# Attention backward: 64-row tiles for scores and dP, a quarter of dS transposed on TensorE, casts on ScalarE

## The chip, the cores and the metric

The kernel runs on one core of a Trainium2 chip. The metric is the device time of one execution in microseconds (us). All times and profiles were taken on the chip. The kernel before took 3544.08 us (median of 2 runs, 3537.90 and 3550.26); its profiled run has a span of 3518.2 us.

In the profile PE is TensorE's matmuls, PEld its weight loads, DVE is VectorE, ACT ScalarE, POOL GpSimd, SP the queue that issues most DMAs. PEclk is the share of full speed that TensorE's clock was granted.

## The reference, cut to what matters

A transformer block (layer norm with modulation, attention with 32 heads of 16, squared-ReLU MLP), forward and backward, for 2048 tokens of width 512. Only the attention backward is changed. Per head, with P the unnormalised exponentials and dO, dP already scaled and shifted by row sums:

```python
S  = Q @ K.T                # scores, recomputed
P  = exp(S * scale)
dP = dO @ V.T               # a row-sum term is folded into two extra columns
dS = P * dP
dV += P.T @ dO;  dK += dS.T @ Q;  dQ += dS @ K
```

## The kernel before

A group g holds four heads, each in a strip of 32 partitions (16 real rows, two more for dP). A unit is two heads (a = 0, 1), 128 queries and 512 keys; there are 1024 units. The scores of one head are taken by a full 128-row matmul against a K tile in which only that head's strip is non-zero ("masked"). dQ needs dS transposed, which a DMA does for two units at a time (DMA_TRANSPOSE in the trace, median 2.60 us; called the crossbar here).

```python
for a in range(2):      # PE, 4 matmuls of 512 columns per unit
    nc.tensor.matmul(sts[a][:], lhsT=T["QT"][:, q], rhs=masked["KT"][2*jp+a][:, c0:c0+512], start=True, stop=True)
for a in range(2):
    nc.tensor.matmul(dp[:, a, :], lhsT=T["dOT"][:, q], rhs=masked["VT"][2*jp+a][:, c0:c0+512], start=True, stop=True)
for a in range(2):      # ACT
    nc.scalar.activation(pu[:, a, :], sts[a][:], ACT.Exp, scale=self.scale)
if len(pend) >= LAG:
    kv(pend.pop(0))     # PE, of two units earlier: 16 matmuls of 16 columns into acckv (dK, dV)
nc.vector.tensor_tensor(ds2[:, i], dp[:], pu[:], ALU.mult)      # DVE
# ... after two units (i = 0, 1):
nc.sync.dma_start_transpose(dsT[:], ds2[:].rearrange("p i a k -> p (i a k)"))   # crossbar
dq(pendq.pop(0))        # PE, of three pairs earlier: 16 matmuls of 16 columns into accq (dQ)
```

PSUM holds two score banks, two dP buffers of two banks, one bank for dK/dV, one for dQ. The order in which each engine issues its instructions is chosen by a scheduler at build time from what is written; it is fixed when the kernel runs.

The softmax here doesn't subtract the row's maximum and nothing guards it: scores larger than these inputs give would overflow.

## Time and profile before

From the page: first the busy tenths of TensorE and the granted clock in 40 slices of the span, then three groups (line, engine, operation, output<-input, shapes, count | busy us, mean ns | idle time before, and what ended it).

```profile
...
PE   5999998888876878487997979989799998999977
...
PEclk7999999999997989699998989999899999999998
...
L1172 ACT ACTIVATE pu<-st 128x512 bf16<-128x512 f32 x2048 | 1114.5, 594 | 573.7 <-PE st L1165 572.3
L1175 DVE TENSOR_TENSOR ds<-dp,pu 128x1024 bf16<-128x1024 f32 x1024 | 1245.8, 1222 | 391.1 <-ACT pu L1172 251.2
...
L1165 PE MATMUL st<-KTm,QTq 128*128 128x512 bf16 x2048 | 655.2, 384 | 8.0 <-issue 6.8
...
```

The backward attention is slices 19 to 38. The clock stands at 8 or above in all but three of the 40 slices. The next fence is the view by stretches for the whole stage (first to last exp) and for a regular part of it: microseconds, busy time and count of each engine, granted clock, DMA share, GB/s.

```profile
...
core 0: us, PE busy (x) PEld busy (x) DVE busy (x) ACT busy (x) POOL busy (x), PEclk, DMA share, GB/s
1648.00:3336.00 1688.00, 1536.60 (x28076) 1013.63 (x28584) 1295.67 (x1243) 1114.17 (x2048) 30.79 (x33) 0.97 1.08 173
2604.40:2619.40 15.00, 14.74 (x277) 9.89 (x280) 12.25 (x10) 10.85 (x21) 0.00 (x0) 1.00 1.20 188
...
```

The stage takes 1688 us, 1.65 us a unit, with TensorE busy 91% of it. In the regular stretch TensorE is busy 14.74 of 15.00 us. The view of waits shows what makes up the rest: waiting for the crossbar's dsT.

```profile
...
PEld L1139 <- DMA dsT<-ds: 162.4, 101, 9.0
PE accq L1139 <- DMA dsT<-ds: 122.4, 87, 8.1
...
```

The timeline of TensorE gives the cost of each piece from start to start:

```profile
...
2603.00 0.59 PE L1165 MATMUL st<-KTm,QTq 128*128 128x512 bf16 x2
2603.43 0.38 PE L1168 MATMUL dp<-VTm,dOTq 128*128 128x512 bf16 x1
2603.86 0.17 PE L1120 MATMUL acckv<-Qg,ds 128*128 128x16 bf16 x1
2603.88 0.17 PE L1122 MATMUL acckv<-dOg,pu 128*128 128x16 bf16 x1
...
```

Two scores start at 2603.00 and the first dP at 2603.43, so a 512-column matmul takes 0.215 us; the second dP of this unit has no record (the trace of before lacks 509 of its 2048 dP matmuls), which is why the next line stands 0.43 us on. The 16-column matmuls follow each other every 25 ns. Four of the first kind and 24 of the second (16 for dK/dV; 8 for dQ, counted at 27 ns) make 0.86 + 0.62 = 1.48 us a unit. The written duration (0.17 us) spans some seven such starts, so it is not what one costs.

| before | us a unit |
|---|---|
| stage / 1024 | 1.65 |
| TensorE, sum of start distances | 1.48 |
| crossbar, 2.9 us for two units | 1.45 |
| VectorE, one product | 1.22 |
| ScalarE, two exps | 1.09 |

### The profile page before, as it was taken

The page shows a single profiled execution, that of the slowest core. Times are in us where ns is not written, and L with a number is a line of the kernel's source. Part 1 is how long each engine was busy: PE and PEld are TensorE (multiplying, and loading weights), DVE is VectorE, ACT ScalarE, POOL GpSimd, SP SyncE. Part 2 cuts the span into 40 slices and gives each one's busy share as a digit, 9 for nine tenths or more (in the row PEclk, how much of TensorE's full clock was granted, in tenths as well). Part 3 has the DMA queues.
Part 4 walks back from the last instruction along what each step waited for, and adds up shares of the span by engine and source line. Part 5 has one row for each costly group of instructions (what it writes and reads, how often), then busy time and mean ns, then how long its engine had stood idle before and what let it go on. Part 6 is the DMA issues. An engine that isn't in the chain of part 4 may idle for free. (4 is left out here: it accounts for less than half of the span.)

```text
span 3518.2 us, 99351 instructions
## 1 busy us (share of the span) xinstructions
PE 3006.1 (85%) x42822; PEld 1747.5 (50%) x43588; DVE 1908.0 (54%) x2886; ACT 2347.3 (67%) x3545; POOL 251.4 (7%) x343
## 2 busy tenths in 40 slices
PE   5999998888876878487997979989799998999977
PEld 2455543333333333265664656656566665666633
DVE  6222220000004366355886868878687786888855
ACT  3999999999982334333765756756566675767633
POOL 3111110000001014311000000000000000000000
PEclk7999999999997989699998989999899999999998
DMA  3111110000013355655999999999999999999952
GB/s 119 63 50 50 45 38 12 12 6 12 5 49 139 113 196 192 189 154 131 174 179 155 178 162 172 176 174 175 161 175 183 176 178 159 180 178 173 176 185 65
DMA packets 1190469, 449.43 MB, mean 128 GB/s; under 512 B 1097354, under 2 KB 1161484, under 8 KB 1190028
## 3 DMA queue, kind: packets, MB, share of 16 engines
q1 hardware_dynamic: 1159900, 361.61, 57.5%
q0 software_dynamic: 21504, 71.71, 6.9%
q10 hardware_dynamic: 8624, 9.70, 0.8%
q8 instruction: 341, 5.59, 0.6%
q14 instruction: 100, 0.82, 0.1%
HBM read 106.83 MB, written 67.64 MB: 50 GB/s over the span
## 5 line engine op out<-in xcount | busy, mean ns | idle before, releaser
L1172 ACT ACTIVATE pu<-st 128x512 bf16<-128x512 f32 x2048 | 1114.5, 594 | 573.7 <-PE st L1165 572.3
L1175 DVE TENSOR_TENSOR ds<-dp,pu 128x1024 bf16<-128x1024 f32 x1024 | 1245.8, 1222 | 391.1 <-ACT pu L1172 251.2
L412 ACT ACTIVATE pu<-st 128x1024 bf16<-128x1024 f32 x1024 | 940.1, 1376 | 4.7 <-PE accbank L418 4.7
L1165 PE MATMUL st<-KTm,QTq 128*128 128x512 bf16 x2048 | 655.2, 384 | 8.0 <-issue 6.8
L409 PE MATMUL st<-QTm,KTq 128*128 128x512 bf16 x1864 | 566.7, 377 | 6.9 <-ACT pu L412 1.5
L1120 PEld LDWEIGHTS <-ds 128*128 128x128 bf16 x8192 | 502.4, 96 | 119.0 <-issue 8.3
L1120 PE MATMUL acckv<-Qg,ds 128*128 128x16 bf16 x8192 | 532.1, 170 | 25.8 <-issue 2.9
L1122 PE MATMUL acckv<-dOg,pu 128*128 128x16 bf16 x8192 | 528.0, 169 | 0.0
L1122 PEld LDWEIGHTS <-pu 128*128 128x128 bf16 x8192 | 460.4, 96 | 118.3 <-issue 8.4
L418 PEld LDWEIGHTS <-pu 128*128 128x128 bf16 x8192 | 291.2, 96 | 458.7 <-ACT pu L412 408.2
L1168 PE MATMUL dp<-VTm,dOTq 128*128 128x512 bf16 x1539 | 508.7, 385 | 0.5 <-DMA dOTq<-dOTq_d 0.5
L418 PE MATMUL accbank<-Vaug,pu 128*128 128x17 bf16 x8192 | 353.5, 172 | 93.4 <-ACT pu L412 38.1
L1139 PE MATMUL accq<-Kg,dsT 128*128 128x16 bf16 x8192 | 311.8, 170 | 125.2 <-DMA dsT<-ds 123.1
L1139 PEld LDWEIGHTS <-dsT 128*128 128x128 bf16 x8192 | 263.5, 96 | 192.4 <-DMA dsT<-ds 164.6
L1168 PEld LDWEIGHTS <-dOTq 128*128 128x128 bf16 x2048 | 188.4, 97 | 244.7 <-issue 81.3
L427 DVE RECIPROCAL rl<-accbank 128x4 f32<-128x4 f32 x128 | 23.0, 180 | 526.0 <-PE accbank L418 525.6
L288 DVE TENSOR_SCALAR ev_fm<-pps,bcol 128x512 bf16<-128x512 f32 x92 | 69.1, 751 | 195.4 <-PE pps L281 185.7
L409 PEld LDWEIGHTS <-KTq 128*128 128x128 bf16 x2048 | 129.7, 96 | 35.4 <-issue 20.5
L1165 PEld LDWEIGHTS <-QTq 128*128 128x128 bf16 x2048 | 128.9, 96 | 11.1 <-issue 8.1
L281 PE MATMUL pps<-xhat1T,wpad 128*128 128x512 bf16 x372 | 119.9, 378 | 7.8 <-DVE ev_fm L288 3.8
L1104 POOL DMA_DIRECT2D QTq<-QTq_d x8 | 4.5, 558 | 1184.0 <-PE dp L1168 1156.4
L544 ACT ACTIVATE rT<-ups,bias 128x512 bf16<-128x512 f32 x56 | 38.5, 687 | 52.1 <-PE ups L542 52.0
(298 smaller groups left out, 2260.2 us busy)
## 6 DMA issues: line engine op xcount, KB each, us to landing
dsT<-ds SPq DMA_TRANSPOSE x512
rT_d<-rT SPq DMA_DIRECT2D x4, 1792.0 KB
rT<-rT_d SPq DMA_DIRECT2D x4, 1792.0 KB
duT_d<-duT POOLq DMA_DIRECT2D x4, 1792.0 KB, 12.0
rT_f<-rT_d SPq DMA_DIRECT2D x14, 512.0 KB
duT_f<-duT_d POOLq DMA_DIRECT2D x14, 512.0 KB, 4.1
xhat_d<-xhat SPq DMA_DIRECT2D x2, 2048.0 KB
QTq_d<-ev_fm POOLq DMA_DIRECT2D x32, 128.0 KB, 2.1
```

The costliest lines, as they stand in the source:

```text
L281: nc.tensor.matmul(pt[:, :sw], lhsT=wpads[t][:, kt, g, :], rhs=xhat1T[:, kt, s0:s0 + sw], start=(kt == 0), stop=(kt == DT - 1))
L288: nc.vector.tensor_scalar(ev[:, :sw], pt[:, :sw], bc, None, ALU.add)
L409: nc.tensor.matmul(stt[:, a, :qw], lhsT=KT[:, kb * P:(kb + 1) * P], rhs=QTm[a][:, q0:q0 + qw], start=True, stop=True)
L412: nc.scalar.activation(pu[:, :, :qw], stt[:, :, :qw], ACT.Exp, scale=self.scale)
L418: nc.tensor.matmul(acc[:, a, sub, :], lhsT=pu[:, a, sub * P:(sub + 1) * P], rhs=Vaug[:, kb, heads[a], :], start=False, stop=False, skip_gr ...
L1120: nc.tensor.matmul(acc[:, 0, a, sub, :], lhsT=ds[:, a, sub * P:(sub + 1) * P], rhs=T["Q"][:, ib, col:col + DH], start=False, stop=False, s ...
L1122: nc.tensor.matmul(acc[:, 1, a, sub, :], lhsT=pu[:, a, sub * P:(sub + 1) * P], rhs=T["dO"][:, ib, col:col + DH], start=False, stop=False, ...
L1139: nc.tensor.matmul(accq[:, ib0 + i, a, :], lhsT=dsT[:, (i * 2 + a) * 4 + sub, :], rhs=T["K"][:, 4 * c + sub, col:col + DH], start=False, s ...
L1165: nc.tensor.matmul(sts[a][:], lhsT=T["QT"][:, q], rhs=masked["KT"][2 * jp + a][:, c0:c0 + 512], start=True, stop=True)
L1168: nc.tensor.matmul(dp[:, a, :], lhsT=T["dOT"][:, q], rhs=masked["VT"][2 * jp + a][:, c0:c0 + 512], start=True, stop=True)
L1172: nc.scalar.activation(pu[:, a, :], sts[a][:], ACT.Exp, scale=self.scale)
L1175: nc.vector.tensor_tensor(ds2[:, i], dp[:], pu[:], ALU.mult)
```

## The change

The intent: TensorE and the crossbar are both nearly full, so relieve both. Scores and dP of a unit use opposite halves of the rows (heads are stored shifted by two strips for dO and V), as two 64-row tiles meant to run side by side. A quarter of the transposes goes from the crossbar to TensorE and VectorE. One dP in five is cast to bf16 by ScalarE, which makes VectorE's product all-bf16. K and V loads leave the transposes' queue.

```diff
-        LAG, LAGQ = 2, 3
+        LAG, LAGQ = 2, 4
 # ... K and V: two zeroed tiles each, by parity of the head, double buffered by group, loaded on the GpSimd queue
+    def turn(u):
+        (ds2, dsT) = u
+        tp = dpp.tile([P, 16, P], BF16, name="dp")          # a dP buffer
+        src = ds2[:].rearrange("p i a (s k) -> p (i a s) k", k=P)
+        for k in range(16):
+            nc.tensor.transpose(tp[:, k, :], src[:, k, :], self.ident[:])
+        nc.vector.tensor_copy(dsT[:], tp[:])
 # ...
+    rs, rd = slice(64 * jp, 64 * jp + 64), slice(64 * (1 - jp), 64 * (1 - jp) + 64)
     for a in range(2):
-        nc.tensor.matmul(sts[a][:], lhsT=T["QT"][:, q], rhs=masked["KT"][2 * jp + a][:, c0:c0 + 512], ...)
-    for a in range(2):
-        nc.tensor.matmul(dp[:, a, :], lhsT=T["dOT"][:, q], rhs=masked["VT"][2 * jp + a][:, c0:c0 + 512], ...)
+        nc.tensor.matmul(sts[a][:], lhsT=T["QT"][rs, q], rhs=T["KT", a][rs, ck], start=True, stop=True)
+        nc.tensor.matmul(dp[:, a, :], lhsT=T["dOT"][rd, q], rhs=T["VT", a][rd, ck], start=True, stop=True)
 # ...
-    nc.vector.tensor_tensor(ds2[:, i], dp[:], pu[:], ALU.mult)
+    if nu % 5 == 2:
+        nc.scalar.copy(ca[:], dp[:])
+        nc.vector.tensor_tensor(ds2[:, i], ca[:], pu[:], ALU.mult)
+    else:
+        nc.vector.tensor_tensor(ds2[:, i], dp[:], pu[:], ALU.mult)
 # ...
-    nc.sync.dma_start_transpose(dsT[:], ...)
+    while pendt: turn(pendt.pop(0))
+    if nt % 4 == 3: pendt.append((ds2, dsT))
+    else: nc.sync.dma_start_transpose(dsT[:], ...)
 # ... in kv(): the matmul with pu now stands ahead of the one with ds
```

## The prediction

> **What bounds it now.** The first and last ScalarE exp of the backward attention start at 1648 and 3335 us, so this stage holds 1024 units (two heads x 128 queries x 512 keys) in 1688 us: 1.65 us each, 48% of the span. Everything else is unchanged by the diff. In that window (view by stretches) TensorE is busy 91%, VectorE 77%, ScalarE 66%, and the DMA engines are full (share 1.08).
> Two limits lie close together. In the regular stretch 2604 to 2619 us a pair of units takes 3.00 us and TensorE is busy 98%: from start distances in the timeline, four 512-column matmuls at 0.215 us, 16 dK/dV matmuls at 25 ns and 8 dQ matmuls at 27 ns give 1.48 us a unit. The other limit is the crossbar: one transpose of a pair's dS holds the queue 2.9 us of those 3.0 (2.60 median), and the masked K/V loads, 0.3 to 0.5 us each, share that queue. When it falls behind, TensorE waits: 123 us plus 165 us of weight loads wait for dsT (view of waits; they overlap), which makes 1.65 out of 1.48.

> **What the change does, per unit.**
> - DMA: a quarter of the transposes and all masked loads leave this queue: 2.9 x 0.75 / 2 = 1.1 us. No longer a limit; the waits for dsT should almost vanish.
> - TensorE: [...]Score and dP use opposite 64-row halves, but only neighbours in the issue order can overlap. In the order of the built kernel the 4096 such matmuls fall into 1444 runs: 344 alternate fully, some 250 are SS,DD (half the gain), over 700 hold only scores or only dP. In-order overlap saves 0.23 us of 0.86. Transposes add 16 x 56 ns (eight take 0.61 us in the feed-forward stage) per 8 units: +0.11.[...]
> - VectorE: 0.8 x 1.245, plus 0.2 x 0.7 for all-bf16 products (estimate from 0.43 us at 512 columns), plus about 1.2/8 to evacuate transposes (0.69 us at 1024 columns), plus 0.07 of small work: 1.36.
> - ScalarE: 1.09 + 0.2 x 1.0 = 1.3.

> So all three engines come to 1.3 to 1.5 us, and the order of two shallow PSUM rings, one of them also lent to the transposes, costs something: I expect 1.50 us a unit, about 150 us less in the stage, nearly all of it on the critical path.

> **Prediction:** 3390 us (range 3270 to 3530). Faster by over 2%: 0.72; within 2%: 0.16; slower: 0.12.

> **What the profile would show.** Waits of TensorE for dsT fall from 288 us to under 80; DMA share in the stage falls from 1.08 to about 0.85; in alternating runs S and D start within about 20 ns of each other, and other runs stay at 0.215 us per matmul;[...] VectorE is 85 to 92% busy, ScalarE 80 to 88%; the stage takes about 1535 us.

> **What would make it wrong.**[...] The transposes hold a dP buffer through matmuls and copy and can stall the dP ring once in eight units. The first group's loads move to the GpSimd queue and may delay the start by some us.

Cut from it are statements that no trace or run of this case had shown, and with them terms of the sum. TensorE's terms that are left come to 1.48 - 0.23 + 0.11 = 1.36 us a unit; the cut term is my guess at what changing between 64-row and 128-row matmuls costs, and with it the sum came to about the 1.50 us a unit of the forecast. That the two halves overlap, on which the 0.23 rests, was itself an assumption then; the trace after shows it (1069 of the 4096 matmuls start within 30 ns of the one before, near the 1093 that counting opposite neighbours in the issue order gives).

## The result, and the profile after

The changed kernel took 4169.24 us (median of 2 runs, 4168.29 and 4170.18): 17.6% slower, ratio 1.1764 (95% interval 1.1675 to 1.1853). Ratios here are the mean time of one kernel's fast runs over that of the other's of the same rounds, so not quite the ratio of the medians quoted.

The page's lines of the changed kernel that answer to those of before:

```profile
...
PE   5999988888578686999999999999999999999987
...
PEclk8999999999789898555555555555556555555578
...
L1189 ACT ACTIVATE pu<-st 128x512 bf16<-128x512 f32 x2048 | 1125.9, 597 | 998.2 <-PE st L1185 825.6
L1197 DVE TENSOR_TENSOR ds<-dp,pu 128x1024 bf16<-128x1024 f32 x819 | 999.9, 1223 | 497.6 <-ACT pu L1189 263.6
L1185 PE MATMUL st<-KT,QTq 64*128 64x512 bf16 x2048 | 1027.4, 584 | 29.7 <-issue 24.2
...
L1195 DVE TENSOR_TENSOR ds<-ca,pu 128x1024 bf16<-128x1024 bf16 x205 | 141.8, 692 | 324.0 <-ACT ca L1194 324.0
...
L1194 ACT CAST ca<-dp 128x1024 bf16<-128x1024 f32 x205 | 208.3, 1016 | 35.8 <-PE dp L1186 35.6
...
```

The second line is the finding: from slice 17 on the clock row reads 5. The score matmul's mean duration is 584 ns, against 384 before. The exps, products, casts and the all-bf16 product last what was expected of them (597, 1223, 1016 and 692 ns). The stage as a whole, in the same columns as before (busy time PE, PEld, DVE, ACT, POOL, then clock, DMA share, GB/s):

```profile
...
1665.00:3984.00 2319.00, 2304.93 (x30602) 1167.36 (x30602) 1348.74 (x1369) 1304.32 (x2253) 59.87 (x92) 0.55 0.55 97
...
```

2319 us, 2.26 us a unit, at a mean clock of 0.55. TensorE is busy 99% of it, DMA only 0.55. So the relief of the crossbar came as intended: TensorE's waits for dsT shrank from 285 to 18 us. The line below is from the view of what the dQ matmuls waited for: the wait's end, then its microseconds and how often.

```profile
...
  DMA dsT<-ds: 17.7, 6
...
```

And the tiles run side by side as intended. TensorE's timeline, in a stretch at the half clock:

```profile
...
2602.77 0.60 PE L1186 MATMUL dp<-VT,dOTq 64*128 64x512 bf16 x1
2602.78 0.61 PE L1185 MATMUL st<-KT,QTq 64*128 64x512 bf16 x1
2603.17 0.63 PE L1186 MATMUL dp<-VT,dOTq 64*128 64x512 bf16 x1
2603.18 0.63 PE L1185 MATMUL st<-KT,QTq 64*128 64x512 bf16 x1
2603.74 0.19 PE L1132 MATMUL acckv<-dOg,pu 128*128 128x16 bf16 x1
2603.79 0.17 PE L1134 MATMUL acckv<-Qg,ds 128*128 128x16 bf16 x1
...
2604.16 0.17 PE L1134 MATMUL acckv<-Qg,ds 128*128 128x16 bf16 x1
2604.27 0.60 PE L1185 MATMUL st<-KT,QTq 64*128 64x512 bf16 x1
```

Score and dP start 10 ns apart (5 ns is the median of such pairs in the trace), but the 512 columns take twice as long: two neighbouring pairs start 0.40 us apart where it was 0.215. The last pair starts at 2603.18 and the first dK/dV matmul only at 2603.74, and from the last dK/dV matmul (2604.16) to the next score is 0.11 us, where narrow matmuls follow each other every 27 ns: the change between 64-row and 128-row matmuls costs time in both directions (0.56 against 0.40 us, 0.11 against 0.03).

TensorE's work a unit, from start distances of this trace, adds up like this. Of 4096 score and dP matmuls, 1093 are hidden behind a partner, as I counted in the built order (in the trace 1069 start within 30 ns of the one before):

| us a unit | at the full clock | at the half clock |
|---|---|---|
| 3003 places of 512 columns | 0.63 (0.215 each) | 1.20 (0.41 each) |
| 24 narrow matmuls | 0.60 (25 ns) | 0.65 (27 ns) |
| transposes, 2 a unit | 0.11 (56 ns) | 0.21 (107 ns) |
| 1444 round trips between the modes | 0.24 (170 ns) | 0.30 (216 ns) |
| sum | 1.58 | 2.36 |

The measured 2.26 lies close to the right column; the trace's clock records say that 222 us of the stage, in 32 stretches of 3.4 to 17.1 us, ran at the full clock. Weighting the two columns with that share gives 2.25.

### The profile page after: what moved, and what is told of

It reads as the page before. It is cut to its first block, busy times and chain, and to the rows that moved or that the text cites. A ratio compares the mean times of both kernels' runs of the same rounds, so it can differ in the third digit from the quotient of the medians.

```text
span 4166.5 us, 103731 instructions
## 1 busy us (share of the span) xinstructions
PE 3811.6 (91%) x45636; PEld 1904.7 (46%) x45636; DVE 1961.0 (47%) x3014; ACT 2537.5 (61%) x3750; POOL 282.3 (7%) x407
## 5 line engine op out<-in xcount | busy, mean ns | idle before, releaser
L1197 DVE TENSOR_TENSOR ds<-dp,pu 128x1024 bf16<-128x1024 f32 x819 | 999.9, 1223 | 497.6 <-ACT pu L1189 263.6
L1185 PE MATMUL st<-KT,QTq 64*128 64x512 bf16 x2048 | 1027.4, 584 | 29.7 <-issue 24.2
L1186 PE MATMUL dp<-VT,dOTq 64*128 64x512 bf16 x2048 | 1002.9, 587 | 0.0
L1134 PEld LDWEIGHTS <-ds 128*128 128x128 bf16 x8192 | 494.6, 104 | 182.9 <-issue 182.9
L1195 DVE TENSOR_TENSOR ds<-ca,pu 128x1024 bf16<-128x1024 bf16 x205 | 141.8, 692 | 324.0 <-ACT ca L1194 324.0
L1148 PE MATMUL dp<-ident,ds 128*128 128x128 bf16 x2048 | 237.7, 310 | 0.1
L1194 ACT CAST ca<-dp 128x1024 bf16<-128x1024 f32 x205 | 208.3, 1016 | 35.8 <-PE dp L1186 35.6
L1148 PEld LDWEIGHTS <-ds 128*128 128x128 bf16 x2048 | 205.8, 145 | 46.8 <-issue 46.5
L1149 DVE COPY dsT<-dp 128x2048 bf16<-128x2048 bf16 x128 | 156.7, 1224 | 140.1 <-PE dp L1148 131.5
L1185 PEld LDWEIGHTS <-QTq 64*128 64x128 bf16 x2048 | 141.0, 104 | 59.7 <-issue 35.3
L1186 PEld LDWEIGHTS <-dOTq 64*128 64x128 bf16 x2048 | 137.6, 105 | 54.3 <-issue 39.7
```

The lines of the kernel that those rows point to most:

```text
L1134: nc.tensor.matmul(acc[:, 0, a, sub, :], lhsT=ds[:, a, sub * P:(sub + 1) * P], rhs=T["Q"][:, ib, col:col + DH], start=False, stop=False, s ...
L1148: nc.tensor.transpose(tp[:, k, :], src[:, k, :], self.ident[:])
L1185: nc.tensor.matmul(sts[a][:], lhsT=T["QT"][rs, q], rhs=T["KT", a][rs, ck], start=True, stop=True)
L1186: nc.tensor.matmul(dp[:, a, :], lhsT=T["dOT"][rd, q], rhs=T["VT", a][rd, ck], start=True, stop=True)
L1194: nc.scalar.copy(ca[:], dp[:])
```

## The experiments

What lowered the clock? Theory 1: the clock follows how much the array is used, and the overlapped half-height matmuls use it too little. Rival 2: the transposes on TensorE lower it. Rival 3: the mode changes cost the time, and the clock is secondary. Kernels marked "single run" were run once, profiled, beside a run of before on the same chip; effects of 3% and more are read from them; a smaller one is a hint only. e4 and e12 to e15 gave wrong values.

### e1: the tiles alone

The kernel before with the 64-row matmuls and their loads, without transposes on TensorE, without casts, lags as before. Issue order as in before, only score and dP alternate.

```diff
-  if nu % 5 == 2:        # casts
+  if False:
-  if nt % 4 == 3:        # TensorE transposes
+  if False:
```

> The kernel before with only the 64-row score and dP matmuls (and the K/V loads that go with them): no TensorE transposes, no ScalarE casts, the lags and dK/dV order of before. Theory 1 (clock: overlapped 64-row matmuls leave the array too little active, and the granted clock falls to one half): mean clock in the backward attention 0.5 to 0.65, a unit 1.8 to 1.95 us, in all about 3700 to 3850 us. Rival 2 (the PE transposes lower the clock): clock above 0.9, 3300 to 3400 us. Rival 3 (the mode changes alone cost the time, the clock is secondary): clock above 0.9 and about 3500 to 3700 us.

3829.43 us against 3518.04 (single run). The stage:

```profile
...
1663.00:3647.00 1984.00, 1920.16 (x28593) 941.73 (x28592) 1308.89 (x1243) 1119.20 (x2048) 59.22 (x91) 0.50 0.86 147
...
```

Clock 0.50 throughout, 1.94 us a unit. No transpose runs on TensorE in it, so rival 2 falls.

### e2: the same tiles, nothing overlaps

e1 with dO and V loaded into the same half as Q and K.

```diff
-  rd = slice(64 * (1 - jp), 64 * (1 - jp) + 64)
+  rd = slice(64 * jp, 64 * jp + 64)        # dOT and VT loaded with their halves exchanged
```

> As e1, same issue order, same 64-row mode and mode changes, but score and dP of a unit use the same half of the rows, so nothing overlaps. Theory 1a (activity is the time in which anything streams): clock above 0.9 again, matmuls 0.215 us apart, about 3500 to 3650 us, faster than e1 though nothing overlaps. Theory 1b (activity is weighted by rows in use): clock 0.5, a unit near 2.5 us, about 4400 us. Rival 2: clock above 0.9. Rival 3: slower than e1 by the lost overlap at full clock, 0.3 us a unit.

4547.52 us (single run).

```profile
...
1662.00:4362.00 2700.00, 2661.47 (x28559) 1164.02 (x28558) 1310.75 (x1242) 1201.61 (x2048) 63.19 (x98) 0.50 0.60 108
...
```

The matmuls now follow one another 0.40 to 0.43 us apart; TensorE streams 4 x 0.41 of 2.64 us, a larger share than the 0.86 of 1.65 of before, and the clock stays at one half. So time in which something streams is not what counts (theory 1a falls); a matmul over 64 rows counts less than one over 128 (1b). Counted in columns rather than time the case is closer; the windows below settle it.

### e3: every pair twice

e1 with each score and dP matmul issued twice, the second overwriting the first.

```diff
   for a in range(2):
+      for _ in range(2):
           nc.tensor.matmul(sts[a][:], ...); nc.tensor.matmul(dp[:, a, :], ...)
```

> As e1, but every overlapped score/dP pair is issued twice (the second run of each overwrites the first, the result stays right): twice the matmul work. Theory 1: the activity is that of before again, clock above 0.9, a unit about 1.6 us, 3450 to 3650 us: more work, less time than e1. Rivals 2 and 3: slower than e1 by 0.4 us a unit, about 4200 us or more if the clock stays at one half.

3667.18 us (single run): twice the score and dP matmuls, 162 us less than e1, though 17 us above the range expected.

```profile
...
1664.00:3483.00 1819.00, 1749.20 (x32680) 1049.15 (x32680) 1309.72 (x1242) 1113.59 (x2048) 58.47 (x90) 0.98 0.94 161
...
```

The clock is 0.98. This refutes rival 3: the mode changes are nearly the same (the trace of e3 has 1022 runs of 64-row matmuls, that of e1 1226), and the 204 fewer, at 0.2 us each, are some 40 of the 162 us. TensorE's timeline of e3 shows the tiles at the full clock:

```profile
...
2602.17 0.38 PE L1186 MATMUL st<-KT,QTq 64*128 64x512 bf16 x1
2602.17 0.38 PE L1187 MATMUL dp<-VT,dOTq 64*128 64x512 bf16 x1
2602.38 0.38 PE L1186 MATMUL st<-KT,QTq 64*128 64x512 bf16 x1
2602.39 0.38 PE L1187 MATMUL dp<-VT,dOTq 64*128 64x512 bf16 x1
2602.70 0.18 PE L1132 MATMUL acckv<-Qg,ds 128*128 128x16 bf16 x1
2602.73 0.17 PE L1134 MATMUL acckv<-dOg,pu 128*128 128x16 bf16 x1
...
```

Pairs 0.21 us apart, and from the last pair (2602.38) to the first narrow matmul 0.31 us. The medians over the stage: 308 ns against 215 without a mode change, and 102 ns against 25 on the way back: 93 + 77 = 170 ns for the round trip. At the half clock (e1) the same steps take 563 and 107 ns, 136 + 80 = 216 ns beyond the 427 and 27 that before shows at its own half-clock moments.

### e4: less streaming without any tile

The kernel before, 128 rows everywhere, with score and dP matmuls of 256 columns that the consumers read twice.

```diff
-  nc.tensor.matmul(sts[a][:], ..., rhs=masked["KT"][2 * jp + a][:, c0:c0 + 512], ...)
+  nc.tensor.matmul(sts[a][:, :256], ..., rhs=masked["KT"][2 * jp + a][:, c0:c0 + 256], ...)   # dP alike
```

> The kernel before, full 128-row mode, no transposes on TensorE, but score and dP matmuls stream 256 columns instead of 512 and the consumers read those twice (wrong numbers on purpose). Theory 1: less streaming alone lowers the granted clock in the stage to 0.5 to 0.7, with no 64-row tile in it; the time stays about that of before, 3450 to 3600 us. Rivals 2 and 3 (the row tiles' mode changes or the transposes are needed): clock stays above 0.9, TensorE busy under 75% in the stage, and about 3350 to 3500 us.

3737.66 us (single run), later than expected; the product was also split in two here.

```profile
...
1642.00:3550.00 1908.00, 1628.37 (x28551) 1295.64 (x28550) 1360.21 (x2262) 1122.75 (x2048) 31.23 (x34) 0.50 0.90 153
...
```

Clock 0.50 without a 64-row matmul or a transpose in the stage. Half the columns do what half the rows did.

### e5: the loads on another queue

The kernel before, its masked loads issued from GpSimd.

```diff
-  nc.sync.dma_start(masked[n][j][r:r + 32, c0:c0 + cw], ...)
+  nc.gpsimd.dma_start(masked[n][j][r:r + 32, c0:c0 + cw], ...)      # backward only
```

> The kernel before, with its masked K and V loads of the backward attention issued from the GpSimd queue instead of the queue of the crossbar transposes. If the transposes fall behind because these loads and their waits block their queue, the waits of TensorE for dsT fall from 288 us to under 150 and the time falls by 50 to 130 us (3410 to 3490). If the crossbar itself is the limit, nothing changes (within 1%).

3528.38 us against 3549.11, ratio 0.9946 (0.9921 to 0.9971). The waits for dsT stayed (176 us of weight loads and 129 us of matmuls in the view of waits, against 165 and 123). The loads on the transposes' queue were not what held it up.

### e6: everything but the tiles

The changed kernel with 128-row masked matmuls.

```diff
-  nc.tensor.matmul(sts[a][:], lhsT=T["QT"][rs, q], rhs=T["KT", a][rs, ck], ...)
+  nc.tensor.matmul(sts[a][:], lhsT=T["QT"][:, q], rhs=masked["KT"][2 * jp + a][:, c0:c0 + 512], ...)   # dP alike
```

> The changed kernel with full 128-row score and dP matmuls (masked operands as before): a quarter of the transposes on TensorE, the casts, the lags and order of the change. Theory 1: clock above 0.9 in the stage; TensorE has 1.48 plus 0.11 us of work a unit, so about the time of before, 3450 to 3600 us. Rival 2: clock near 0.55, 4000 us or more.

3517.22 us against 3549.11, ratio 0.9913 (0.9892 to 0.9934).

```profile
...
1648.00:3330.00 1682.00, 1652.69 (x30622) 1133.68 (x30619) 1322.56 (x1372) 1283.30 (x2253) 31.31 (x35) 0.99 0.79 134
...
```

Clock 0.99. Transposes on TensorE, casts and the new lags are worth 0.9% together; the tiles, with the K and V loads that go with them, are the whole loss.

### e7: the change without TensorE transposes

```diff
-  if nt % 4 == 3:
+  if False:
```

> The changed kernel without the TensorE transposes (all on the crossbar). Theory 1: clock stays 0.5 to 0.65; saves the transposes' 0.2 us a unit at half clock: about 3900 to 4000 us. Rival 2: clock above 0.9, 3400 us or less.

3925.76 us (single run).

```profile
...
1660.00:3738.00 2078.00, 2035.58 (x28565) 961.68 (x28565) 1197.92 (x1242) 1310.73 (x2253) 59.48 (x92) 0.50 0.83 141
...
```

As expected: still the half clock (0.50), and cheaper by 243 us, near the transposes' time there (0.21 us a unit, 215 us).

### e8 and e9: a useless matmul more

The changed kernel with one full-height matmul more per unit, into the bank that the score overwrites; 256 and 512 columns.

```diff
+  nc.tensor.matmul(sts[0][:, :256], lhsT=self.ident[:], rhs=T["QT"][:, 0:256], start=True, stop=True)   # e9: 512
   for a in range(2):
```

> The changed kernel with one useless matmul more per unit: full 128 rows, 256 columns, into the score bank that the real score then overwrites (right result). Activity theory (the granted clock follows columns streamed times rows in use in each 3.4 us window): raised by 256 of about 1660 columns a unit, the stage leaves the half clock for most of the time, clock above 0.85, a unit about 1.5 to 1.6 us, in all 3400 to 3550 us: more work, over 600 us less. If the mode changes were the cost: slower than the changed kernel, 4200 us or more.

> As e8 with a useless matmul of 512 columns. Activity theory: clock above 0.95, a unit 1.6 to 1.7 us, 3480 to 3620 us; slower than e8 if e8 already holds the full clock, faster than e8 if it does not.

e8: 3717.75 us, e9: 3652.26 us (single runs), against 4169 for the change. The stage of e8, then of e9:

```profile
...
1663.00:3534.00 1871.00, 1840.02 (x31637) 1049.03 (x31635) 1338.54 (x1369) 1284.56 (x2253) 59.71 (x91) 0.88 0.70 121
...
```

```profile
...
1662.00:3469.00 1807.00, 1755.52 (x31633) 1009.62 (x31630) 1335.24 (x1369) 1280.90 (x2253) 59.40 (x91) 0.99 0.73 125
...
```

More work, 451 and 517 us less, with the clock at 0.88 and 0.99. Both came out above the expected time: the clock did what theory 1 said, but a unit took 1.83 and 1.76 us where 1.5 to 1.6 and 1.6 to 1.7 were expected. The scheduler also alternates more pairs in these (729 and 856 runs of two overlapped pairs in the traces, against 465 in the changed kernel), so part of the gain may be order; e1, with 862 such runs at the half clock, shows that order alone does not bring the clock back.

### e10: half of the transposes on TensorE

```diff
-  if nt % 4 == 3:
+  if nt % 2 == 1:
```

> The changed kernel with half of dS transposed on TensorE instead of a quarter. If TensorE transposes count as activity: the clock rises clearly over the 0.55 of the changed kernel (0.7 or more in the stage) and the time falls below 4000 us although TensorE has 0.1 to 0.2 us a unit more to do. If transposes do not count as activity: clock at 0.55 or below and 4300 us or more.

4441.99 us (single run).

```profile
...
1662.00:4260.00 2598.00, 2591.94 (x32680) 1371.74 (x32679) 1501.23 (x1497) 1308.43 (x2253) 60.84 (x93) 0.58 0.44 61
...
```

Between the two expectations (0.58 against 0.55), so inconclusive by itself. The windows below decide it.

### e11: e1 with the useless matmul

The line added in e8, put into e1.

> e1 (64-row tiles alone, no TensorE transposes, no casts; it never left the half clock) with the useless 256-column matmul of e8. Activity theory: about 1660 columns a unit, at the half clock some 2900 a window, close to where the clock recovers, so it may stay locked at 0.5 (then about 3950 us) or escape (clock above 0.9, about 3400 to 3500 us, the crossbar then the limit). Mode-change theory: clock 0.5 whatever is added.

3705.52 us (single run) against 3829 for e1.

```profile
...
1664.00:3521.00 1857.00, 1775.52 (x29588) 898.43 (x29588) 1300.61 (x1242) 1116.93 (x2048) 58.97 (x90) 0.71 0.95 158
...
```

The clock escapes, but only in part: 0.71.

### What the clock follows

```
columns x rows/128     window at full clock          window at half clock
in the window          next half   next full         next half   next full
under 2500             163         0                 2254        0
2500 to 3000           112         27                1786        38
3000 to 3500           42          267               259         173
3500 and more          0           4813              1           117
```

A window that holds under 2500 is never followed by the full clock, and one with 3500 or more is followed by it in all but one case of 4931, from either clock. The border lies near 3000 to 3300 columns, against some 8100 that fit (512 in 0.215 us). The best single limit mistakes 59 of the 5424 windows at full clock. If a 64-row matmul is counted at 0.4, 0.5 or 0.6 of a 128-row one, it mistakes 63, 59 and 82; counted in full, 196. If the transposes are left out it mistakes 228, and if the zero columns of e12 to e18 (below) are left out, 144. So rows count, at about one half for 64 of 128, and so do transposes on TensorE and columns of zeros. This also settles e2: without the rows, 155 of its windows hold 3500 columns or more, and none of them is followed by the full clock. Some records are missing (509 dP matmuls in before), which may explain part of the blurred border; what the hardware counts in detail is not shown.

With that, columns per unit explain the stages (sum per unit, over the measured time of a unit, times 3.413):

| kernel | columns a unit | us a unit | columns a window | clock |
|---|---|---|---|---|
| before | 2432 | 1.65 | 5036 | 0.97 |
| after | 1664 | 2.26 | 2508 | 0.55 |
| e1 | 1408 | 1.94 | 2480 | 0.50 |
| e2 | 1408 | 2.64 | 1822 | 0.50 |
| e4 | 1408 | 1.86 | 2579 | 0.50 |
| e11 | 1664 | 1.81 | 3132 | 0.71 |
| e8 | 1920 | 1.83 | 3587 | 0.88 |
| e9 | 2176 | 1.76 | 4209 | 0.99 |
| e3 | 2432 | 1.78 | 4673 | 0.98 |

For before that is 4 x 512 + 24 x 16; for after 4 x 512 / 2 + 24 x 16 + 256 for the transposes. The state feeds itself: at the half clock the changed kernel does not issue enough columns to leave it (2508 a window over the stage). A burst of 16 transposes can lift it: all 32 lifts of the changed kernel follow a window with eight or more transposes, though only one in four of its 128 such windows brings a lift. Then the stretch without transposes falls back.

### e12 to e15: columns at no cost

If columns count, they can be had nearly free: at the full clock a dK/dV matmul starts 25 ns after the last with 16 columns (before) and with 48 (e12). At the half clock it does not come free: 27 ns with 16, 40 ns with 48. Q and dO are kept in tiles with zero columns between the heads, and each matmul streams 48 columns, 32 of them zeros that add nothing to neighbouring accumulators.

```diff
-  nc.tensor.matmul(acc[:, 0, a, sub, :], lhsT=ds[...], rhs=T["Q"][:, ib, col:col + DH], ...)
+  nc.tensor.matmul(o[:, lo * DH:(lo + 3) * DH], lhsT=ds[...], rhs=wideQ[:, ib, r0 * DH:(r0 + 3) * DH], ...)   # dV alike
```

e12 is the change with this, e13 is e1 with this, e14 is e12 without casts, e15 is e12 without TensorE transposes.

> The changed kernel with its dK/dV matmuls made 48 columns wide (16 real ones, 32 zero columns that add nothing; right result). Such a matmul starts 25 to 27 ns after the one before[...]. If activity is columns streamed, zeros too, this raises it by 512 columns a unit at almost no time: clock above 0.9, a unit 1.4 to 1.55 us, 3300 to 3480 us, faster than before. If narrow or zero columns do not count: clock 0.55, about 4100 us.

> e1 (64-row tiles alone) with the 48-column dK/dV matmuls of e12. Activity theory: 1920 columns a unit, clock above 0.8 against 0.50 for e1, at or under 3500 us with the crossbar as the limit (1.45 us a unit). If narrow or zero columns do not count: 0.5 and 3830 us like e1.

> e12 without the ScalarE casts. Clock above 0.9 as e12; VectorE then has 1.245 + 0.15 + 0.07 = 1.47 us a unit, ScalarE 1.09: if the casts are worth what the prediction gave them, 0.03 to 0.1 us a unit slower than e12 (3380 to 3550 us).

> e12 without the TensorE transposes. Clock 0.8 to 1.0; crossbar at 1.45 us a unit is the limit, TensorE has 0.11 us less: 3380 to 3550 us. If transposes on TensorE are what lifts the clock out of its low state, it stays lower than e12's.

All four gave a relative error of 0.11 in the gradient of the QKV weights: I had placed the copy into a padded tile ahead of the last lagged dK/dV matmuls that still read it. Times (single runs; before took 3531.23): e12 3633.18, e13 3589.74, e14 3600.55, e15 3511.10 us. The stage of e12:

```profile
...
1679.00:3452.00 1773.00, 1647.11 (x30609) 1036.46 (x30607) 1316.86 (x1369) 1278.64 (x2253) 74.99 (x106) 0.96 0.74 127
...
```

From 0.55 to 0.96 with not one matmul more in the stage. The clock in the stages of e13, e14, e15 was 0.89, 0.96 and 0.94. e15 is faster than e12 by 122 us: once the clock is full, the transposes on TensorE cost about their 0.11 us a unit (113 us) and buy nothing. e14 is faster than e12 by 33 us, a hint that the casts cost too. The clock was as expected; the times of e12, e13 and e14 lie 153, 90 and 51 us above the ranges expected.

### e16, e17 and e18: right values, and what the other two parts are worth

e16 is e15 with the copy moved behind those matmuls and half of the clearing given to VectorE. e17 puts one transpose of eight on TensorE. e18 is e16 without casts.

```diff
+  if Tn is not None and jp == 0 and c == 1:
+      widen(Tn, g + 1)                # was in load_group
-  if False:                           # e17: if nt % 8 == 7:
-  if nu % 5 == 2:                     # e18: if False:
```

> e15 with its fault mended: the padded copies of Q and dO are now written after the last lagged dK/dV matmuls of the group that used them, so the result must be right; half of the clearing goes to VectorE, so the stage should start some 20 us earlier. Activity theory: clock above 0.9 in the stage as in e15, 3450 to 3520 us, 1 to 2.5% faster than before; the same kernel with 16-column dK/dV matmuls (e7) took 3926 us at the half clock. If the wrong values had anything to do with e15's clock: back to the half clock.

> e16 with one of eight transposes on TensorE. If the crossbar is what still limits e16, the waits of TensorE for dsT fall and it is 1% faster than e16; if the dP buffer lent to the transposes is what made e12 120 us slower than e15, half of that comes back: 50 to 60 us slower than e16.

> e16 without the ScalarE casts. VectorE then has 1.245 + 0.07 = 1.32 us a unit, ScalarE 1.09, the crossbar 1.45 as in e16. If the casts pay once the clock is full, as the prediction had it (0.1 us a unit less on VectorE): 30 us or more slower than e16. If another engine sets the pace: within 20 us of e16. If the wait of VectorE for the cast is what it costs (e14 was 33 us under e12): faster than e16.

All three are correct. e16: 3482.94 us against 3556.59 in the same rounds, ratio 0.9789 (0.9754 to 0.9824). e17: 3508.04, ratio 0.9867 (0.9843 to 0.9891), 25 us slower than e16: half of what was expected of the lent dP buffer, but its direction, and no gain from a relieved crossbar. e18: 3430.62 against 3535.41 in its own rounds, ratio 0.9708 (0.9660 to 0.9756). e16 and e18 ran on different chips and are compared through before, so the gap between their ratios (0.8%, the intervals just touch) leans on the trace: the stage takes 1639 us in e16 and 1580 in e18. The stage of e16, then of e18:

```profile
...
1660.00:3299.00 1639.00, 1492.18 (x28581) 914.54 (x28581) 1173.40 (x1242) 1274.83 (x2253) 76.35 (x108) 0.95 1.14 178
...
```

```profile
...
1658.00:3238.00 1580.00, 1477.87 (x28565) 909.98 (x28564) 1266.89 (x1242) 1110.29 (x2048) 76.25 (x108) 0.95 1.18 185
...
```

e18 is the best version found: 2.9% faster than before, 1.54 us a unit. It keeps the overlapped tiles and drops the other two parts. Not tested is before with the 48-column matmuls, or with e18's loads and lags, but with 128-row matmuls; so how much of the 2.9% the tiles alone bring is not shown (the loads' queue alone gave 0.5%, e5).

## Why the prediction was wrong

It said 3390 us, in a range of 3270 to 3530, with 0.72 for faster. It came out at 4169.

- **The step that failed** is the costing of every TensorE term at the start distances of before: "four 512-column matmuls at 0.215 us", transposes at "56 ns", and in the list of signs that runs without a partner "stay at 0.215 us per matmul". The changed kernel's took 0.40 us and its transposes 107 ns, because the granted clock fell from 0.97 to 0.55. The clock is not in the prediction's list of what could go wrong either. The change gives TensorE fewer columns times rows in each window, and that is what lowered the clock (2508 a window against 5036; e1, e2 and e4; e3, e8, e9 and e12 in the other direction).
- **What failed beside it.** With the clock held at 0.96, e12 (values wrong, single run) still takes 1.73 us a unit and 3633 us, slower than before and 243 us above the prediction. So about 540 of the 779 us missed go with the clock. The prediction took the unit to be about as long as TensorE's sum, 1.50 us. The sum at the full clock is 1.58 us, with 0.24 for mode changes, 0.1 more than the guessed term, and in e12 TensorE is busy 1.61 of 1.73 us, so 0.12 us of waiting is left. What makes that waiting is only in part taken apart (e15, e17, e18).
- **Overlap of the tiles: right.** Pairs start 5 ns apart (median); 1093 of 4096 matmuls are hidden by the built order, as predicted, and 1069 in the trace. What the overlap hides at the half clock (0.44 us a unit at 0.41 each) is no more than what doubling the others costs (3003 x 0.195 us over 1024 units = 0.57).
- **Mode changes: a cost was expected, its size was off.** e3 gives 93 and 77 ns at the full clock, 0.085 us on average, more than I had guessed; why a change takes that time is not shown. The difference alone is 0.1 us a unit, and would have stayed inside the range.
- **Crossbar: right.** Waits for dsT fell to 18 us (under 80 predicted). DMA share fell to 0.55, not 0.85, only because the stage grew.
- **VectorE and ScalarE terms: right** in each duration (692 ns for the bf16 product, 1224 for the evacuation of a transpose, 1016 for a cast; the other product takes 1.22 us, not 1.245), but "all three engines come to 1.3 to 1.5 us" did not follow: TensorE had 2.26, the others were 58 and 56% busy.
- **The value of the parts.** I counted the transposes and casts as part of the gain. Beside 128-row matmuls they gain 0.9% together (e6); beside overlapped tiles at the full clock they lose: e17 is 25 us slower than e16 with an eighth of the transposes, and e18, without the casts, has a stage 59 us shorter than e16. Why the casts cost is not shown; VectorE waits for the cast in the view of waits (171 us in e16).

## What to carry to other kernels

In these runs TensorE's clock was a result of the program (0.97 in the stage before, 0.55 after, 0.95 in e18), not a constant: before halving the columns or the rows that a stage streams, work out columns times rows per 3.4 us window and compare it with what the trace shows to be enough (here some 3300 of 8100). When a faster form of a matmul makes a stage slower, read the granted clock of the stage first; if it has dropped, widen narrow matmuls whose start distance at the full clock does not grow with it (25 ns with 16 and with 48 columns here; 27 and 40 ns at the half clock) before giving up the form. Zero columns served for that: e7 at 16 columns took 3926 us at clock 0.50, e16 at 48 columns 3483 us at 0.95 (e16's padded copies, their buffers and the clearing are the only other differences). And test each part of a bundle alone: here one part held all of the loss and, once the clock was held, the best version was the one that kept this part and dropped the others.
